# A linear-attention kernel fused with a mixture-of-experts block: the opening put in hand order on four engines, with dummy products, and the loop's order of work rewritten

## The chip, the cores and the metric

The kernel runs on one core of one Trainium2 chip. Times are device microseconds (us) of one execution. Repeated executions of one kernel mostly agree within about 0.5%. Each execution has a state, fast or slow (slow: more than 1.5% above the fastest of its kernel). A "span" is the time from the first to the last instruction in the one execution that was profiled; it is 1.5 to 2 us shorter than that execution's time.

## The reference

RWKV-6 attention over four sequences, eight heads, 768 positions and head size 48. Its output, as 3072 rows of 384, goes through a two-layer block with a squared ReLU.

```python
def _attn_ref(r, k, v, w, u):
    state = zeros(B, H, D, D)
    for t in range(S):
        kt, vt, rt, wt = k[:, :, t], v[:, :, t], r[:, :, t], w[:, :, t]
        cur = einsum('bhd,bhe->bhde', u[None] * kt, vt)
        y[:, :, t] = einsum('bhd,bhde->bhe', rt, state + cur)
        state = wt[:, :, :, None] * state + einsum('bhd,bhe->bhde', kt, vt)
    return y

def _moe_ref(x, w_in, w_out):          # 3072x384, 384x2048, 2048x384
    r = np.maximum(x @ w_in, 0.0)
    return (r * r) @ w_out
```

## The kernel before

The attention is cut into 24 steps of 128 positions (six per sequence). A step is a chain across engines, and the letters name its TensorE parts:

- `c`: sums of the logarithms of w. ScalarE takes `Ln` before and `Exp` after it, then VectorE multiplies r and k by the result (`rdec`).
- `t`: transposes of `rdec`, copied out by VectorE (`rkT`).
- `p`: products of keys and receptances, masked by VectorE (`pmT`).
- `s`: the state update, finished by VectorE and GpSimd.
- `y`: the step's output. VectorE adds the bonus term `vq` (`y_sb`).
- `x`: transposes of `y_sb`, copied by ScalarE into `xT`, the input of the second part.

Beside the chain GpSimd makes the bonus: `ku`, `qprod`, then VectorE's reduction `q`, then `vq` again on GpSimd. It needs the step's k from memory, and nothing in the step needs it before `y_sb`.

The block behind it ("MoE" in the code) is cut into units, and `F` puts one into the order of TensorE. A first-layer unit, called A here, is six products of 256 columns; ScalarE takes it out of PSUM (`rl`) and VectorE squares it (`gt`). A second-layer unit, called B, is four products of 384 columns; after four B units ScalarE takes the sum out of PSUM (`o_sb`). Either unit takes TensorE about 0.655 us (0.66 us for an A and 0.65 us for a B from one start to the next, at 158.35 us in the timeline of the steady loop below). There are 192 of them. A has two PSUM buffers, B has one; `cp` and `y` (one buffer of 2 x 512 columns each) and `tr` (one) are the rest.

```python
    ps_m1 = ctx.enter_context(tc.tile_pool(name="ps_m1", bufs=2, space=PSUM))
    ps_m2 = ctx.enter_context(tc.tile_pool(name="ps_m2", bufs=1, space=PSUM))
    # ... cut ...
    def fill(_):                                   # the F of the order
        if not fills and coming:
            fills.extend(coming.popleft()[1])      # a new block, before its time
        if not fills and held and flush[0]:
            fills.extend(held.popleft())           # second-layer units alone
        if fills:
            fills.popleft()()
        if coming:
            coming[0][0] -= 1
            if coming[0][0] <= 0:                  # LAG = 2 fills after its x
                fills.extend(coming.popleft()[1])

    def finish(step):                              # the x of the order
        st_yt(step)
        if step in blocks:
            m1s, m2s = moe_block(*blocks[step])
            old = held.popleft() if held else []
            held.append(m2s)
            units = []
            for i in range(max(len(m1s), len(old))):
                units += m1s[i:i + 1] + old[i:i + 1]   # A B A B ...
            coming.append([LAG, units])
    # ... cut ...
    with tc.manual_schedule(engines={nc.tensor.engine}):
        st_prep(0)
        run("c0 t0 p0 s0 i0 c1 i1 y0 t1 x0 p1 s1 i2 y1 i3 x1 O0 O1 O2 O3")
        ahead(PF - 1)
        run("F F F F F F c2 F F t2 o0 p2 s2 o1 y2 o2 x2 o3 F F F F F F F F c3 F F F F t3 s3")
        flush[0] = False
        for t in range(3, NSTEP):
            f = ["F F"] * 4 if t > 8 else ...      # cut: fewer in the first steps
            run(f"c{t + 1} {f[0]}" + (f" x{t - 1}" if t > 3 else "") +
                f" {f[1]} t{t + 1} p{t} {f[2]} s{t + 1} {f[3]} y{t}")
        run(f"F F x{NSTEP - 1}")
        flush[0] = True
        while fills or held or coming:
            fill(0)
```

Only TensorE runs in the order of the text; the order of VectorE, ScalarE and GpSimd is chosen automatically when the kernel is built. The loop is pipelined by a step: `c`, `t` and `s` of step t+1 stand beside `p` and `y` of step t. And `flush[0] = False` keeps second-layer units back until there are first-layer units to alternate with.

## Time and profile before

| | |
|---|---|
| time, median of 4 executions (range) | 233.99 us (233.26 to 234.39) |
| span, mean granted clock of TensorE | 232.5 us, 0.955 |
| TensorE busy, 120 to 190 us | 69.78 of 70 us |
| steady period of a step (start of `rdec`, steps 10 to 22) | 7.49 us |
| start of `y_sb` of step 8, of step 23 | 96.8 us, 209.1 us |

The page cuts the span into 40 slices of 5.8 us. Each digit is a busy share in tenths, and the second line is the granted clock of TensorE in tenths of full speed:

```profile
PE   0145694794787999989999999999999999999984
PEclk9999997589569999999999999999999999999999
DMA  7999998999999999998785561010001000101001
```

TensorE has holes for 80 us, in which the loads bring the digit of the DMA engines to 7 to 9, and then almost none. The table of windows gives the same by stage. Its columns are the stretch, its length, busy time of PE (TensorE), PEld (its weight loads), DVE (VectorE), ACT (ScalarE) and POOL (GpSimd) with the count of instructions, the granted clock, the DMA share and GB/s:

```profile
0.00:45.00 45.00, 21.62 (x203) 15.05 (x204) 18.12 (x35) 24.65 (x34) 14.69 (x27) 0.92 1.04 244
45.00:60.00 15.00, 11.57 (x109) 8.18 (x108) 6.40 (x13) 7.20 (x15) 8.87 (x10) 0.84 1.17 183
60.00:84.00 24.00, 19.30 (x249) 13.79 (x249) 17.40 (x33) 12.31 (x26) 12.88 (x16) 0.83 1.13 198
84.00:120.00 36.00, 34.56 (x407) 25.56 (x403) 29.24 (x55) 22.65 (x47) 19.31 (x22) 1.00 0.97 177
120.00:190.00 70.00, 69.78 (x813) 51.71 (x809) 54.43 (x99) 45.48 (x94) 24.93 (x30) 1.00 0.24 57
```

So up to about 84 us there is something to win for TensorE, and afterwards the kernel is as good as its work. Two lines each of the timelines of ScalarE, VectorE and TensorE show the opening. The columns are start, length, engine, line, operation, and in brackets the idle time before it and who ended it:

```profile
6.66 0.51 ACT L151 CAST v_bf<-v_raw 128x384 bf16<-128x384 f32 x1 [4.64 <-DMA v_raw<-in_v_dram]
7.08 0.52 ACT L149 ACTIVATE lw_buf_149<-w_raw 128x384 bf16<-128x384 f32 x1
...
10.15 0.55 DVE L160 TENSOR_REDUCE q<-qprod 128x8 f32<-128x384 f32 x1 [7.64 <-POOL qprod L158]
10.62 0.94 DVE L177 TENSOR_TENSOR rdec_buf_155<-rk_raw,cp 128x768 bf16<-128x768 f32 x1
...
26.52 1.44 PE L272 MATMUL m_370<-xT,wi_sb 128*128 128x256 bf16 x6 [0.57 <-ACT xT L256]
...
32.10 0.82 PE L272 MATMUL m_420<-xT,wi_sb 128*128 128x256 bf16 x6
```

The first `Ln` stands behind a cast of v that waited for its load. The first `rdec`, which the whole chain waits for, stands behind a bonus reduction that nobody needs yet (this alone costs 0.2 us, as its `Exp` ended at 10.41 us). The first A units run at about half speed: the first takes 1.44 us, and the next two start 1.28 us apart (27.75 and 29.03 us), against 0.82 us at 32.10 us and 0.66 us from one start to the next in the loop. In the steady loop, A and B alternate (L272 is A, L287 is B), with no idle time in brackets:

```profile
158.35 0.82 PE L272 MATMUL m_2601<-xT,wi_sb 128*128 128x256 bf16 x6
159.01 0.81 PE L287 MATMUL m_2549<-wo_sb,gt 128*128 128x384 bf16 x4
159.66 0.33 PE L255 MATMUL tr<-ident,y_sb 128*128 128x128 bf16 x3
159.82 0.82 PE L272 MATMUL m_2620<-xT,wi_sb 128*128 128x256 bf16 x6
160.48 0.81 PE L287 MATMUL m_2549<-wo_sb,gt 128*128 128x384 bf16 x4
```

### The profile page before, as it was taken

Reading aid. Unit: us, or ns where it says so; the run is one execution under the profiler, and the core shown is the slowest. Engines: PE = TensorE matmul, PEld = TensorE weight load, DVE = VectorE, ACT = ScalarE, POOL = GpSimd, SP = SyncE. Lnnn points to the kernel's source line nnn. Section 1 sums busy time; section 2 is a strip of 40 time slices with the busy share of each in tenths; the row PEclk is TensorE's granted clock in tenths of the full one; section 3 lists DMA queues with packets and bytes.
Section 4 is the critical chain, followed back from the end, with each engine's and each line's share of the span. In section 5 each row is a group of like instructions: output and inputs, shape, how many; then the busy total and the mean of one; then the engine's idle time right before and its main releaser. Section 6 shows DMA issues by size and latency. Waiting matters only on the chain.

```text
span 232.5 us, 5432 instructions
## 1 busy us (share of the span) xinstructions
PE 194.8 (84%) x2120; PEld 141.3 (61%) x2120; DVE 143.0 (61%) x264; ACT 131.4 (57%) x249; POOL 81.2 (35%) x105
## 2 busy tenths in 40 slices
PE   0145694794787999989999999999999999999984
PEld 0023472663465677767777777777777777777742
DVE  2244356235567688796879878987677756753210
ACT  2338479274245558547655775567755664455530
POOL 4450410547525855357626563431211120000000
PEclk9999997589569999999999999999999999999999
DMA  7999998999999999998785561010001000101001
GB/s 137 206 344 280 327 295 163 190 171 189 187 206 216 174 199 194 220 184 166 141 167 113 110 126 37 34 36 3 35 34 38 35 3 34 37 34 37 34 34 68
DMA packets 107176, 30.42 MB, mean 131 GB/s; under 512 B 100368, under 2 KB 105616, under 8 KB 107152
## 3 DMA queue, kind: packets, MB, share of 16 engines
q1 hardware_dynamic: 107152, 30.09, 63.0%
q8 instruction: 16, 0.26, 0.5%
q14 instruction: 8, 0.07, 0.1%
HBM read 25.36 MB, written 4.72 MB: 129 GB/s over the span
## 4 chain that ended last, share of the span: by engine, by line
PE 56%; SPq 14%; DVE 8%; DMA 7%; POOL 6%; issue 4%; ACT 3%; POOLq 0%; DVEq 0%; ACTq 0%
SPq L68 13%; PE tr L188 4%; DMA rk_raw<-in_k_dram 4%; PE cp L220 2%; DVE pmT L223 2%; POOL qprod L158 2%; POOL ku L157 2%; DVE rkT L189 2%; DMA u_bc<-in_u_dram 2%; DMA v_raw<-in_v_dram 2%; DVE gt L277 1%; PE y L234 1%; PE tr L255 1%; PE cp L171 1%; PE m_3691 L287 1%
## 5 line engine op out<-in xcount | busy, mean ns | idle before, releaser
L277 DVE TENSOR_TENSOR gt<-rl 128x512 bf16<-128x512 f16 x96 | 48.1, 509 | 34.2 <-ACT rl L276 33.8
L272 PEld LDWEIGHTS <-wi_sb 128*128 128x128 bf16 x624 | 57.2, 102 | 15.4 <-issue 3.4
L287 PEld LDWEIGHTS <-gt 128*128 128x128 bf16 x384 | 37.4, 99 | 18.6 <-issue 2.7
L208 POOL TENSOR_TENSOR S<-t_state,a_c 128x192 bf16<-128x192 f32 x20 | 10.5, 525 | 72.6 <-DVE t_state L206 56.3
L223 DVE TENSOR_TENSOR pmT<-cp,tri_strict 128x512 bf16<-128x512 f32 x48 | 30.7, 679 | 2.5 <-PE cp L220 2.5
L162 POOL TENSOR_TENSOR vq<-v_raw,q 128x384 f32<-128x384 f32 x24 | 20.0, 833 | 32.8 <-DVE y_sb L245 18.9
L160 DVE TENSOR_REDUCE q<-qprod 128x8 f32<-128x384 f32 x24 | 13.2, 549 | 21.5 <-POOL qprod L158 13.9
L157 POOL TENSOR_TENSOR ku<-rk_raw,u_bc 128x384 f32<-128x384 f32 x24 | 24.4, 1018 | 4.6 <-DMA u_bc<-in_u_dram 4.6
L158 POOL TENSOR_TENSOR qprod<-rk_raw,ku 128x384 f32<-128x384 f32 x24 | 24.4, 1018 | 3.1 <-DVE q L160 1.3
L151 ACT CAST v_bf<-v_raw 128x384 bf16<-128x384 f32 x24 | 12.2, 510 | 15.4 <-PE y L234 8.8
L189 DVE COPY rkT<-tr 128x1024 bf16<-128x1024 bf16 x24 | 16.4, 685 | 5.7 <-PE tr L188 5.4
L175 ACT ACTIVATE cp<-cp 128x768 f32<-128x768 f32 x24 | 19.2, 799 | 0.5 <-DVE q L160 0.2
L245 DVE TENSOR_TENSOR y_sb<-vq,y 128x384 bf16<-128x384 f32 x24 | 13.2, 551 | 2.2 <-PE y L234 1.1
L256 ACT COPY xT<-tr 128x384 bf16<-128x384 bf16 x24 | 11.4, 476 | 3.4 <-PE tr L255 3.3
L220 PE MATMUL cp<-rkT 64*128 64x128 bf16 x192 | 10.6, 237 | 3.0 <-DVE rkT L189 3.0
L234 PEld LDWEIGHTS <-pmT 128*128 128x128 bf16 x192 | 8.9, 101 | 6.8 <-DVE pmT L223 4.4
L234 PE MATMUL y<-v_bf,pmT 128*128 128x48 bf16 x192 | 10.6, 191 | 2.8 <-DVE pmT L223 2.7
L177 DVE TENSOR_TENSOR rdec_buf_159<-rk_raw,cp 128x768 bf16<-128x768 f32 x8 | 7.6, 952 | 6.5 <-ACT cp L175 5.1
L255 PE MATMUL tr<-ident,y_sb 128*128 128x128 bf16 x72 | 8.6, 234 | 2.4 <-DVE y_sb L245 1.6
L220 PEld LDWEIGHTS <-rkT 64*128 64x128 bf16 x192 | 6.0, 101 | 6.2 <-DVE rkT L189 3.4
L188 PE MATMUL tr<-ident,rdec_buf_157 128*128 128x128 bf16 x64 | 5.7, 242 | 4.7 <-DVE rdec_buf_157 L177 4.7
L255 PEld LDWEIGHTS <-y_sb 128*128 128x128 bf16 x72 | 6.0, 103 | 5.9 <-DVE y_sb L245 2.8
(295 smaller groups left out, 362.8 us busy)
## 6 DMA issues: line engine op xcount, KB each, us to landing
w_raw<-in_w_dram SPq DMA_DIRECT2D x24, 192.0 KB, 4.4
rk_raw<-in_r_dram SPq DMA_DIRECT2D x24, 192.0 KB, 4.5
rk_raw<-in_k_dram SPq DMA_DIRECT2D x24, 192.0 KB, 4.6
v_raw<-in_v_dram SPq DMA_DIRECT2D x24, 192.0 KB, 4.0
out_dram<-o_sb SPq DMA_DIRECT2D x24, 192.0 KB, 2.0
w_st<-in_moe_w_in_dram SPq DMA_DIRECT2D x4, 768.0 KB, 8.0
w_st<-in_moe_w_out_dram SPq DMA_DIRECT2D x4, 768.0 KB, 9.3
u_bc<-in_u_dram SPq DMA_DIRECT2D x1, 192.0 KB, 4.2
```

Source lines behind the costliest of these rows:

```text
L68: nc.sync.dma_start(out=dst, in_=src[b, :, c * C:(c + 1) * C, :].rearrange("h c d -> c h d"))
L157: nc.gpsimd.tensor_mul(ku[:], st["rk_raw"][:, 1], u_bc[:])
L158: nc.gpsimd.tensor_mul(qprod[:], st["rk_raw"][:, 0], ku[:])
L162: nc.gpsimd.tensor_mul(vq[:], st["v_raw"][:], q[:, :, None].to_broadcast([C, H, D]))
L175: nc.scalar.activation(cs[:, :, 0:DM], cs[:, :, 0:DM], AF.Exp)
L189: nc.vector.tensor_copy(rkT[:], ps_tr[:])
L220: nc.tensor.matmul(ps_p[:, e, p * C:(p + 1) * C], rkT[rows, 1, p, :], rkT[rows, 0, p, :], start=True, stop=True)
L223: nc.vector.tensor_mul(pmT[:, e], ps_p[:, e].rearrange("p (a t) -> p a t", a=HP), tri_strict[:, None, :].to_broadcast([C, HP, C]))
L234: nc.tensor.matmul(ps_y[:, e, p * D:(p + 1) * D], st["pmT"][:, e, p, :], st["v_bf"][:, 2 * p + e, :], start=(p == 0), stop=(c == 0), skip_ ...
L272: nc.tensor.matmul(ps1[:, j, :], wi_sb[:, kk, n * 128:(n + 1) * 128], xT[:, kk, t0:t0 + width], start=(kk == 0), stop=(kk == KT - 1))
L277: nc.vector.tensor_mul(hold["gt"][:, g * ng:(g + 1) * ng, :], rl[:], rl[:])
L287: nc.tensor.matmul(ps2[:], gt[:, n, mt * 128:(mt + 1) * 128], wo_sb[:, n, :], start=(n == 0), stop=(n == NT - 1))
```

## The change

The intent was to shorten the opening. VectorE, ScalarE and GpSimd are put in hand order too for steps 0 to 3. The casts of the weights are cut into slices and shared by ScalarE (`i`, `o`) and VectorE (`I`, `O`). TensorE's idle time is filled with 43 dummy products (`W`), meant to keep its clock up. MoE blocks of the steps 2, 3, 4 and 23 cover one step. Two things come along with this in the loop: it is no longer pipelined by a step, and the `flush` flag is gone, so second-layer units are used as soon as the fills run empty.

```diff
-    def cast_wi(g):
-        nc.scalar.copy(wi_sb[:, :, g * GW:(g + 1) * GW], w_st.pop(("i", g))[:])
+    def cast(dst, src, by_act):
+        for j in range(dst.shape[1]):
+            if by_act:
+                nc.scalar.copy(dst[:, j], src[:, j])
+            else:
+                nc.vector.tensor_copy(dst[:, j], src[:, j])
 # ... cut: the old cast_wo; cast_wi and cast_wo now call cast; st_prep is split into st_lw (l) and st_v (v), st_bonus into st_bonus (b)
 #     and st_q (q), st_cum into st_cum (c) and st_rd (r), one letter each ...
-    blocks = {1: (0, 256), 2: (2 * C, 128), 3: (3 * C, 128)}
-    for step in range(5, NSTEP, 2):
+    blocks = {1: (0, 256)}
+    for step in range(2, NLEAD):                    # NLEAD = 5
+        blocks[step] = (step * C, 128)
+    for step in range(NLEAD + 1, NSTEP, 2):
         blocks[step] = ((step - 1) * C, 256)
+    if (NSTEP - NLEAD) % 2:
+        blocks[NSTEP - 1] = ((NSTEP - 1) * C, 128)
-    flush = [True]
-        if not fills and held and flush[0]:
+        if not fills and held:
             fills.extend(held.popleft())
+    def keep_warm(n):
+        ps = ps_m2.tile([C, 512], FP32, name="m2")
+        for _ in range(n):
+            nc.tensor.matmul(ps[:], warm[:, 0:C], warm[:], start=True, stop=True)
-    # ... cut: the opening and the loop shown above ...
+    with tc.manual_schedule(engines={E.PE}):
+        with tc.manual_schedule(engines={E.DVE, E.Activation, E.Pool}):
+            run("W10 l0 c0 r0 v0 b0 W6 t0 W2 q0 p0 l1 s0 W2 y0 W1 c1 b1 x0 r1 v1 W6 t1"
+                " W2 q1 p1 i0 s1 W2 y1 W2 x1 I1 F i2 F F I3 F J0 F F l2 c2 F F b2 r2 v2"
+                " J1 J2 J3 H4 W4 t2 W2 q2 p2 o0 s2 W2 y2 W2 x2 O1 F F F F o2 F F O3 F l3 c3"
+                " F F b3 r3 v3 F F t3 F q3 p3 F s3 F y3 l4")
+        for t in range(4, NSTEP):
+            f = FEW if t < NFEW else "F F;F F;F F;F;F".split(";")   # FEW: 6 fills, t < 8
+            run(f"c{t} r{t} b{t} H{t + PF - 1} {f[0]} x{t - 1} v{t} {f[1]} t{t} q{t} {f[2]}"
+                f" p{t} {f[3]} s{t} {f[4]} y{t}" + (f" l{t + 1}" if t + 1 < NSTEP else ""))
```

More of the change, by code (lines that the diff above doesn't have):

```diff
@@ L46 @@
     LAG = 2
+    NLEAD = 5
+    NFEW = 8
+    FEW = "F;F;F F;F;F".split(";")
     nc.scalar.preload_act_table_set("natural_log_exp_and_others")
@@ L97, in load_wo, with cast_wi, cast_wo, load_u @@
             in_=moe_w_out[g * 512:(g + 1) * 512, :].rearrange("(a p) d -> p a d", p=128))
-    def cast_wi(g):
-        nc.scalar.copy(wi_sb[:, :, g * GW:(g + 1) * GW], w_st.pop(("i", g))[:])
-    def cast_wo(g):
-        nc.scalar.copy(wo_sb[:, g * 4:(g + 1) * 4, :], w_st.pop(("o", g))[:])
-    loads = {0: attn_load(0)}
-    u_bc = consts.tile([C, H, D], FP32)
-    nc.sync.dma_start(
-        out=u_bc[:],
-        in_=bass.AP(tensor=u.tensor, offset=u.offset,
-                    ap=[[0, C]] + [list(x) for x in u.ap]))
-    loads[1] = attn_load(1)
+    def cast(dst, src, by_act):
[4 more added lines that the diff above has]
+                nc.vector.tensor_copy(dst[:, j], src[:, j])
+    def cast_wi(g, by_act):
+        cast(wi_sb[:, :, g * GW:(g + 1) * GW], w_st.pop(("i", g)), by_act)
+    def cast_wo(g, by_act):
+        cast(wo_sb[:, g * 4:(g + 1) * 4, :], w_st.pop(("o", g)), by_act)
+    loads = {}
+    u_bc = consts.tile([C, H, D], FP32)
+    def load_u():
+        nc.sync.dma_start(
+            out=u_bc[:],
+            in_=bass.AP(tensor=u.tensor, offset=u.offset,
+                        ap=[[0, C]] + [list(x) for x in u.ap]))
+    def load_step(step):
+        loads[step] = attn_load(step)
+    load_step(0)
+    load_u()
+    load_step(1)
     for g in range(4):
         load_wi(g)
-    loads[2] = attn_load(2)
+    load_step(2)
     tri_strict = consts.tile([C, C], BF16)
@@ L125 @@
     nc.vector.memset(ones_col[:], 1.0)
+    warm = consts.tile([C, 512], BF16)
+    nc.vector.memset(warm[:], 0.0)
     NLW = 3
@@ L142, with st_lw, st_v @@
     S_of = {}
-    def st_prep(step):
-        ld = loads.pop(step)
-        st = states[step] = dict(ld)
+    def st_lw(step):
+        st = states[step] = dict(loads.pop(step))
         lw = st["lw"] = lw_bufs[step % NLW]
-        nc.scalar.activation(lw[:, :, 0:D], ld["w_raw"][:], AF.Ln)
+        nc.scalar.activation(lw[:, :, 0:D], st["w_raw"][:], AF.Ln)
+    def st_v(step):
+        st = states[step]
         v_bf = st["v_bf"] = a_mid.tile([C, H, D], BF16, name="v_bf", bufs=3)
-        nc.scalar.copy(v_bf[:], ld["v_raw"][:])
+        nc.scalar.copy(v_bf[:], st["v_raw"][:])
     def st_bonus(step):
@@ L155, in st_bonus, with st_q @@
         ku = a_mid.tile([C, H, D], FP32, name="ku")
-        qprod = a_mid.tile([C, H, D], FP32, name="qprod")
+        qprod = st["qprod"] = a_mid.tile([C, H, D], FP32, name="qprod")
         nc.gpsimd.tensor_mul(ku[:], st["rk_raw"][:, 1], u_bc[:])
         nc.gpsimd.tensor_mul(qprod[:], st["rk_raw"][:, 0], ku[:])
+    def st_q(step):
+        st = states[step]
         q = a_small.tile([C, H], FP32, name="q")
-        nc.vector.reduce_sum(q[:], qprod[:], axis=AX.X)
+        nc.vector.reduce_sum(q[:], st["qprod"][:], axis=AX.X)
         vq = st["vq"] = a_mid.tile([C, H, D], FP32, name="vq", bufs=3)
@@ L166, in st_cum @@
         lw = st["lw"]
-        cs = ps_cp.tile([C, 2, 512], FP32, name="cp")
+        cs = st["cs"] = ps_cp.tile([C, 2, 512], FP32, name="cp")
         for p in range(HP):
@@ L175, in st_cum, with st_rd @@
         nc.scalar.activation(cs[:, :, 0:DM], cs[:, :, 0:DM], AF.Exp)
+    def st_rd(step):
+        st = states[step]
         rdec = st["rdec"] = rdec_bufs[step % NRD]
@@ L178, in st_cum @@
             rdec[:, :, :, 0:D], st["rk_raw"][:],
-            cs[:, :, 0:DM].rearrange("p a (h d) -> p a h d", h=H))
+            st.pop("cs")[:, :, 0:DM].rearrange("p a (h d) -> p a h d", h=H))
     def st_tr(step):
@@ L335, in ahead @@
         while asked[0] <= min(last, NSTEP - 1):
-            loads[asked[0]] = attn_load(asked[0])
+            load_step(asked[0])
             asked[0] += 1
-    def cum(step):
-        if step < NSTEP:
-            st_cum(step)
-            if step + 1 < NSTEP:
-                st_prep(step + 1)
-            if step > 1:
-                ahead(step + PF)
-    def tr(step):
-        if step < NSTEP:
-            st_tr(step)
-            st_bonus(step)
-    def su(step):
-        if step < NSTEP:
-            st_su(step)
-    ops = {"c": cum, "t": tr, "p": st_p, "s": su, "y": st_y, "x": finish,
-           "F": fill,
-           "i": cast_wi, "o": cast_wo, "O": load_wo}
+    ops = {"l": st_lw, "v": st_v, "c": st_cum, "r": st_rd, "b": st_bonus, "q": st_q,
+           "t": st_tr, "p": st_p, "s": st_su, "y": st_y, "x": finish, "F": fill,
+           "W": keep_warm, "J": load_wo, "H": ahead,
+           "i": lambda g: cast_wi(g, True), "I": lambda g: cast_wi(g, False),
+           "o": lambda g: cast_wo(g, True), "O": lambda g: cast_wo(g, False)}
     def run(text):
@@ L362, in run @@
             ops[tok[0]](int(tok[1:] or 0))
-    with tc.manual_schedule(engines={nc.tensor.engine}):
-        st_prep(0)
-        run("c0 t0 p0 s0 i0 c1 i1 y0 t1 x0 p1 s1 i2 y1 i3 x1 O0 O1 O2 O3")
-        ahead(PF - 1)
-        run("F F F F F F c2 F F t2 o0 p2 s2 o1 y2 o2 x2 o3 F F F F F F F F c3 F F F F t3 s3")
-        flush[0] = False
-        for t in range(3, NSTEP):
-            f = ["F F"] * 4 if t > 8 else ["F F", "F F", "F F", "F"] if t > 5 else ["F"] * 4 if t == 3 else ["F", "", "F", ""]
-            run(f"c{t + 1} {f[0]}" + (f" x{t - 1}" if t > 3 else "") +
-                f" {f[1]} t{t + 1} p{t} {f[2]} s{t + 1} {f[3]} y{t}")
+    E = mybir.EngineType
+    with tc.manual_schedule(engines={E.PE}):
+        with tc.manual_schedule(engines={E.DVE, E.Activation, E.Pool}):
+            run("W10 l0 c0 r0 v0 b0 W6 t0 W2 q0 p0 l1 s0 W2 y0 W1 c1 b1 x0 r1 v1 W6 t1"
[3 rows of a table added]
+        for t in range(4, NSTEP):
+            f = FEW if t < NFEW else "F F;F F;F F;F;F".split(";")
+            run(f"c{t} r{t} b{t} H{t + PF - 1} {f[0]} x{t - 1} v{t} {f[1]} t{t} q{t} {f[2]}"
+                f" p{t} {f[3]} s{t} {f[4]} y{t}" + (f" l{t + 1}" if t + 1 < NSTEP else ""))
         run(f"F F x{NSTEP - 1}")
-        flush[0] = True
         while fills or held or coming:
```

## The prediction

> **What bounds the kernel now.** Two regimes. From 120 to 209 us TensorE is busy 88.8 of 89 us (table of windows), about 7.55 us per step of 128 rows. Before 83.7 us it is busy only 52.2 us, partly at half clock: six products of a MoE block took 1.44-1.49 us until 30 us and 0.82 us later; the granted clock of 40-50 and 60-70 us was 0.61 and 0.58. DMA is saturated until about 106 us (page, slices); from 36 us on a step's loads are issued every 4.0-4.5 us and land 4.0-4.6 us later: step 3 is complete at about 40 us, step 4 at 44, step 6 at 52-53.
>
> **What the change does.** (1) Hand order for VectorE, ScalarE, GpSimd in steps 0-3: the first Ln no longer stands behind the cast of v (6.66 us), the first rdec product no longer behind the reduction q (10.15 us). Following the chain with the trace's durations, rdec of step 0 starts near 7.5 instead of 10.6, the first MoE product near 21 instead of 26.5, the transposed rows of step 2 come near 35 instead of 42. (2) Dummy products, 43 of 512 columns, keep TensorE warm[...]. They sit in gaps and save 4-6 us of cold MoE. (3) Single-step blocks for steps 2-4 and 23 cost nothing: 12 products of 128 columns were spaced 0.67 us, six of 256 columns 0.66. A halved last block saves 0.6 us of tail. (4) Casts keep their total. (5) Fills: 45 MoE units come ahead of step 8 instead of 32; 13 x 0.655 = 8.5 us moved into the opening.
>
> **What takes some back.** After step 3 VectorE's built order has the reductions q of steps 4, 5 and 6 ahead of rdec of step 4. q of step 6 needs its k (landed about 52), then ku, S, qprod (2.5 us on GpSimd): rdec of step 4 cannot start before about 55 us (before: 57.2), with a TensorE hole of some 4 us[...]. The early lead is largely lost to DMA; the fills done in it stay. Second, the steady order is no longer pipelined by one step, and fills come as eight first-layer units, then eight second-layer ones. In the first-layer stretch VectorE has 8 us of work per 7.5 us; between p and y stand 1.6 us of TensorE work for a 1.3 us mask product, and a unit waits for its evictor behind the 0.8 us Exp. I estimate 0.2-0.5 us lost per step, 3-8 us in 16 steps.
>
> **Sum.** 8.5 (fills) + 1.2 (attention products of step 7 already done) + 2 (rdec of step 4) + 0.6 (tail) less about 4 = 8 us off 234.3.
>
> **Prediction: 226 us, 219 to 231 eight times in ten. Faster by over 2%: 0.76; within 2%: 0.21; slower: 0.03.**
>
> **What would show it.** First MoE product at 20-22 us, six in 0.8 us; rdec of step 4 at 53-57 us, released by q or k of step 6, after a TensorE hole; step period after step 8 of 7.6-8.0 us, with waits on relu evictions and masked products (pmT); last attention product near 209 us or later, then a MoE tail of 13 us instead of 20.
>
> **What would make it wrong.** k of step 6 earlier, or no steady stalls (then 219). Or the eight-and-eight fills stall more than 0.5 us a step, or outputs in the DMA queue hold back loads (then over 230).

That dummies keep TensorE fast was not yet shown by a run then; hl_nowarm below gives the measure, and the 4 to 6 us put on it were the estimate from before's trace (six products in 1.44 to 1.49 us instead of 0.82, clock 0.61 and 0.58).

## The result and the profile after

| | before | after |
|---|---|---|
| time, median (range) | 233.99 us (233.26 to 234.39) | 236.82 us (236.54 to 237.22) |
| span, mean granted clock | 232.5 us, 0.955 | 235.2 us, 0.993 |
| first A unit, six products | 26.52 us, 1.44 us long | 20.21 us, 0.81 us long |
| steady period of a step | 7.49 us | 8.11 us |
| start of `y_sb` of step 8, of step 23 | 96.8, 209.1 us | 95.1, 217.4 us |

The ratio is 1.013 (95% interval 1.009 to 1.016). A ratio here is the mean time of a kernel's fast executions over that of the fast executions of the kernel before in the same rounds, so it is not quite the ratio of the medians quoted. The change made the kernel 1.3% slower, clear of the noise but within 2%, on a predicted gain of 3.4%. All outputs, here and in every experiment below, agree with the reference.

The page's slices and the windows of after answer to those above:

```profile
PE   7776768497987788989989989999989999999984
PEclk9999999979999999999999999999999999999999
```

```profile
0.00:45.00 45.00, 32.98 (x297) 18.44 (x301) 25.40 (x52) 21.91 (x44) 17.05 (x29) 1.00 1.00 243
...
60.00:84.00 24.00, 19.16 (x264) 13.74 (x264) 19.60 (x33) 13.02 (x27) 14.01 (x16) 1.00 1.13 195
...
120.00:190.00 70.00, 65.49 (x728) 47.27 (x727) 50.16 (x93) 42.98 (x88) 21.10 (x26) 1.00 0.35 73
```

The first row has 33 us of TensorE work in place of 22, part of it dummies. The clock is what the change wanted: from 60 to 84 us it is 1.00, where it was 0.83. The last row is what nobody wanted. TensorE is idle for 4.51 us of 70, where it was idle for 0.22 us before. The view of waits, for TensorE from 120 to 190 us, lists nothing for before. For after it lists these among others (total, times, longest, in us; L299 is A, L314 is B):

```profile
PE y L261 <- DVE pmT L250: 0.5, 2, 0.3
PE m_2028 L299 <- ACT rl L303: 0.5, 1, 0.5
PE m_2618 L299 <- ACT rl L303: 0.5, 1, 0.5
...
PE cp L247 <- DVE rkT L216: 0.4, 2, 0.2
PE m_2688 L314 <- ACT o_sb L318: 0.3, 1, 0.3
```

The timeline of TensorE over one step shows where they stand:

```profile
153.21 0.82 PE L299 MATMUL m_2591<-xT,wi_sb 128*128 128x256 bf16 x6
153.86 0.82 PE L299 MATMUL m_2601<-xT,wi_sb 128*128 128x256 bf16 x6
154.52 0.33 PE L282 MATMUL tr<-ident,y_sb 128*128 128x128 bf16 x3
155.32 0.82 PE L299 MATMUL m_2618<-xT,wi_sb 128*128 128x256 bf16 x6 [0.47 <-ACT rl L303]
155.97 0.81 PE L314 MATMUL m_2628<-wo_sb,gt 128*128 128x384 bf16 x4
...
160.29 0.81 PE L314 MATMUL m_2688<-wo_sb,gt 128*128 128x384 bf16 x4 [0.34 <-ACT o_sb L318]
```

A units now come together, eight of A and then eight of B, because every step consumes exactly the eight units that it makes, the queue of fills runs empty in between, and without the flag an empty queue is filled with B units alone. The third A of the stretch shown needs a PSUM buffer that ScalarE has not emptied (0.47 us). The fifth B in a row needs the only B buffer (0.34 us). With the alternating order of before, each buffer had a unit of the other kind in which to be emptied.

The second new thing lies between 42 and 57 us. The first fence is ScalarE's timeline and the second TensorE's; the third is VectorE's a little later:

```profile
44.84 0.52 ACT L167 ACTIVATE lw_buf_155<-w_raw 128x384 bf16<-128x384 f32 x1 [1.85 <-DMA w_raw<-in_w_dram]
...
45.46 0.80 ACT L199 ACTIVATE cp<-cp 128x768 f32<-128x768 f32 x1
46.16 0.49 ACT L318 ACTIVATE o_sb<-m_601 128x384 f32<-128x384 f32 x1
```

```profile
43.48 0.81 PE L314 MATMUL m_601<-wo_sb,gt 128*128 128x384 bf16 x4
46.70 2.80 PE L314 MATMUL m_688<-wo_sb,gt 128*128 128x384 bf16 x12 [2.41 <-ACT o_sb L318]
```

```profile
54.40 0.55 DVE L272 TENSOR_TENSOR y_sb<-vq,y 128x384 bf16<-128x384 f32 x1 [0.34 <-PE y L268]
56.59 0.55 DVE L184 TENSOR_REDUCE q<-qprod 128x8 f32<-128x384 f32 x1 [1.64 <-POOL qprod L179]
57.06 0.95 DVE L204 TENSOR_TENSOR rdec_buf_159<-rk_raw,cp 128x768 bf16<-128x768 f32 x1
```

The `Ln` at 44.84 us writes the third of the three buffers in turn, whose earlier use was step 2, so it belongs to step 5. It waited 1.85 us for step 5's w, and the `Exp` of step 3 at 45.46 us stood behind it, though its products were done by 43.7 us (from TensorE's timeline). The B sum that had to leave PSUM stood behind both, hence TensorE's hole of 2.41 us. The reduction at 56.59 us is `q` of step 6, read from the built order of VectorE. It waited 1.64 us, with `rdec` of step 4 behind it, whose `Exp` had ended at 55.99 us: `rdec` itself was held for 1.07 us. The load wasn't what came last here: step 6's k had landed at 52.0 us, but GpSimd, busy with `vq` and `qprod` of earlier steps, began `ku` at 54.14 us. In these fences both engines ran their instructions in the order in which they stand: the `Exp` began only behind the `Ln` that had waited 1.85 us, and `rdec` only behind the reduction that had waited 1.64 us. In both the automatic order of the loop has put an operation of a later step, which isn't ready (on ScalarE it waits for a load, on VectorE for GpSimd), ahead of one that TensorE needs now. The hand order of the opening did not keep it out: hand-ordered instructions keep their order among themselves, and here an automatic one (the `Ln` of step 5 at 44.84 us) stands between them, ahead of the `Exp` of step 3.

### A ledger of the lead

Since one kernel is pipelined and the other not, `rdec` of the same step is not the same point of progress. The addition `y_sb` is. With the count of MoE units that stand ahead of it in TensorE's order (counted in the program text, fills that find nothing left out), the profiled executions give:

| kernel | `y_sb` of step 8 | units ahead of it | step 8 to 23 (120 units) | step 23 to the end | span |
|---|---|---|---|---|---|
| before | 96.8 us | 44 | 112.3 us | 23.4 us | 232.5 us |
| after | 95.1 us | 53 | 122.4 us | 17.8 us | 235.2 us |

At step 8 after was 1.7 us and 9 units ahead; at 0.655 us a unit that is a lead of 7.6 us. It then lost 10.1 us in the steady loop, and its end was 5.6 us shorter for the 9 units already done. The sum is -1.7 + 10.1 - 5.6 = 2.8 us, and the spans differ by 2.7 us.

Even `y_sb` is not quite the same point. The pipelined kernel has done `c`, `t` and `s` of the next step by then, except at step 23, which has no next one. These take TensorE 1.1 us (0.44, 0.45 and 0.24 us from one start to the next in after, 151 to 158 us). So after's lead at step 8 is rather 6.5 us and its steady loss 9.0 us; the sum stays the same. The period agrees: 15 steps of 0.63 us are 9.4 us.

### The profile page after: what moved, and what is told of

It reads as the page before. It is cut to its first block, busy times and chain, and to the rows that moved or that the text cites. A ratio compares the mean times of both kernels' runs of the same rounds, so it can differ in the third digit from the quotient of the medians.

```text
span 235.2 us, 5615 instructions
## 1 busy us (share of the span) xinstructions
PE 201.6 (86%) x2208; PEld 138.8 (59%) x2211; DVE 151.1 (64%) x279; ACT 127.2 (54%) x255; POOL 81.3 (35%) x105
## 4 chain that ended last, share of the span: by engine, by line
PE 49%; DVE 16%; issue 11%; POOL 8%; ACT 8%; DMA 5%; SPq 3%; POOLq 0%; DVEq 0%; ACTq 0%
DVE pmT L250 6%; DVE gt L304 4%; PE tr L215 3%; POOL ku L178 3%; POOL qprod L179 3%; ACT rl L303 3%; DMA rk_raw<-in_r_dram 3%; PE cp L247 3%; SPq L71 3%; ACT o_sb L318 2%; DVE rkT L216 2%; DMA u_bc<-in_u_dram 2%; PE y L261 2%; PE cp L195 1%; PE y L268 1%
## 5 line engine op out<-in xcount | busy, mean ns | idle before, releaser
L299 PEld LDWEIGHTS <-wi_sb 128*128 128x128 bf16 x672 | 56.6, 97 | 19.1 <-issue 9.6
L304 DVE TENSOR_TENSOR gt<-rl 128x512 bf16<-128x512 f16 x96 | 49.3, 529 | 16.2 <-ACT rl L303 15.8
L314 PEld LDWEIGHTS <-gt 128*128 128x128 bf16 x384 | 35.7, 98 | 26.9 <-issue 8.3
L250 DVE TENSOR_TENSOR pmT<-cp,tri_strict 128x512 bf16<-128x512 f32 x48 | 31.7, 685 | 6.6 <-PE cp L247 6.5
L186 POOL TENSOR_TENSOR vq<-v_raw,q 128x384 f32<-128x384 f32 x24 | 20.0, 833 | 30.3 <-DVE y_sb L272 14.3
L204 DVE TENSOR_TENSOR rdec_buf_157<-rk_raw,cp 128x768 bf16<-128x768 f32 x8 | 7.6, 950 | 10.1 <-ACT cp L199 10.1
L247 PE MATMUL cp<-rkT 64*128 64x128 bf16 x192 | 9.5, 219 | 3.1 <-DVE rkT L216 3.1
L247 PEld LDWEIGHTS <-rkT 64*128 64x128 bf16 x192 | 5.4, 94 | 10.7 <-DVE rkT L216 7.6
L198 ACT ACTIVATE a_c<-cp 128x4 f32<-128x4 f32 x24 | 4.1, 173 | 13.5 <-PE cp L196 13.5
L204 DVE TENSOR_TENSOR rdec_buf_159<-rk_raw,cp 128x768 bf16<-128x768 f32 x8 | 7.6, 949 | 3.9 <-ACT cp L199 3.9
L204 DVE TENSOR_TENSOR rdec_buf_161<-rk_raw,cp 128x768 bf16<-128x768 f32 x8 | 7.6, 948 | 2.0 <-ACT cp L199 2.0
```

Of the source, the lines that this page charges most:

```text
L186: nc.gpsimd.tensor_mul(vq[:], st["v_raw"][:], q[:, :, None].to_broadcast([C, H, D]))
L204: nc.vector.tensor_mul(rdec[:, :, :, 0:D], st["rk_raw"][:], st.pop("cs")[:, :, 0:DM].rearrange("p a (h d) -> p a h d", h=H))
L247: nc.tensor.matmul(ps_p[:, e, p * C:(p + 1) * C], rkT[rows, 1, p, :], rkT[rows, 0, p, :], start=True, stop=True)
L250: nc.vector.tensor_mul(pmT[:, e], ps_p[:, e].rearrange("p (a t) -> p a t", a=HP), tri_strict[:, None, :].to_broadcast([C, HP, C]))
L299: nc.tensor.matmul(ps1[:, j, :], wi_sb[:, kk, n * 128:(n + 1) * 128], xT[:, kk, t0:t0 + width], start=(kk == 0), stop=(kk == KT - 1))
L304: nc.vector.tensor_mul(hold["gt"][:, g * ng:(g + 1) * ng, :], rl[:], rl[:])
```

## The experiments

Each edit is against after unless it says otherwise. "Before" was run again beside each group, with medians of 233.9 to 234.4 us. Groups ran on different chips, so that times of different groups compare less well than their ratios. All results are of timed rounds; periods and single lines are of one profiled execution. Each kernel has four timed executions; hold_lag, hand_all and hand_pipe had one slow one each, which is left out of their ratios and medians. hand_all's profile is of the slowest of its three fast executions (240.0 us at a mean granted clock of 0.985; the others took 236.8 and 237.0 us at 0.998 and 1.000). Its windows show a clock of 0.50 from 12.6 to 15.9 us and from 46.7 to 50.0 us (six dummy products took 2.58 us at 13.67 us; in outq the same six took 1.46 us), so lines of its opening come later than in the others; in the loop, from 120 to 190 us, its clock was 1.00.

| kernel | median us | ratio to before (95%) | steady period us | `y_sb` of step 8 | step 8 to 23 |
|---|---|---|---|---|---|
| after | 236.8 | 1.013 (1.009 to 1.016) | 8.11 | 95.1 | 122.4 |
| hold | 243.5 | 1.041 (1.033 to 1.049) | 8.29 | 93.3 | 125.2 |
| pipe | 238.7 | 1.019 (1.014 to 1.024) | 8.15 | 96.7 | 121.3 |
| pipe_hold | 234.7 | 1.001 (0.994 to 1.008) | 7.68 | 97.0 | 113.3 |
| oldopen | 239.4 | 1.022 (1.017 to 1.027) | 8.11 | 96.3 | 122.8 |
| hold_lag | 233.4 | 0.998 (0.992 to 1.004) | 7.70 | 89.8 | 116.8 |
| outq | 241.7 | 1.034 (1.032 to 1.037) | 8.03 | 98.0 | 122.7 |
| hand8 | 242.9 | 1.039 (1.036 to 1.042) | 8.19 | 97.8 | 124.8 |
| nowarm | 237.8 | 1.018 (1.012 to 1.023) | 8.12 | 94.5 | 122.8 |
| hand_all | 237.0 | 1.016 (1.008 to 1.024) | 8.50 | 92.5 | 127.7 |
| hand_lag | 226.0 | 0.965 (0.961 to 0.969) | 7.49 | 86.0 | 113.8 |
| hand_pipe | 225.5 | 0.965 (0.959 to 0.972) | 7.49 | 89.6 | 110.5 |
| cap | 232.7 | 0.995 (0.987 to 1.003) | 7.61 | 91.2 | 115.6 |
| hl_oldopen | 231.1 | 0.988 (0.986 to 0.990) | 7.50 | 92.0 | 113.9 |
| bef_hand | 230.6 | 0.986 (0.983 to 0.989) | 7.48 | 94.4 | 110.5 |
| hl_nowarm | 229.2 | 0.983 (0.977 to 0.988) | 7.50 | 90.0 | 113.9 |

### Is it the bursts, or the loop that is no longer pipelined?

The main theory for the steady loss was that units of one kind in a burst wait for their evictor. The rival was that the loop, no longer pipelined by a step, leaves too little between `p`, the mask and `y`. The first three kernels change one or both.

**hold** brings the flag back and leaves the rest of after:

```diff
-        if not fills and held:
+        if not fills and held and flush[0]:
             fills.extend(held.popleft())
 # and, around the loop:
+        flush[0] = False
         for t in range(4, NSTEP):
 # ...
         run(f"F F x{NSTEP - 1}")
+        flush[0] = True
```

> The changed kernel, but from step 4 on second-layer MoE units are held back until the next block's first-layer units can be alternated with them, as in the kernel before; the attention order stays unpipelined. Theory burst (eight first-layer units in a row overload VectorE and ScalarE): the period between the rdec products of steps 10 and 22 falls from 8.11 to about 7.6 us. Theory order (no pipelining by a step, so short distances p to y and c to t): it stays at 8.0 or more. Total is muddied by the backlog that alternation needs (some empty fills in steps 5 to 9): 228 to 236 under burst, 236 to 242 under order.

It was the slowest of all, 243.5 us. The waits on PSUM are nearly gone, but another has come. The view of waits for TensorE, 120 to 190 us:

```profile
PE m L299 <- ACT xT L283: 4.9, 4, 1.2
PE m L314 <- ACT o_sb L318: 0.6, 3, 0.2
```

Every second step the fills run out just before `x`, and the first A unit of the new block stands directly behind the transposes whose copy `xT` it needs: 1.2 us each time. Before still has units left at that point, and `LAG` puts two of them in between. So alternation needs a backlog, and after has used it up.

**pipe** restores the pipelined order and keeps the bursts:

```diff
-        for t in range(4, NSTEP):
-            f = FEW if t < NFEW else "F F;F F;F F;F;F".split(";")
-            run(f"c{t} r{t} b{t} H{t + PF - 1} {f[0]} x{t - 1} v{t} ... y{t} l{t + 1}")
+        cnt = {3: (1, 1, 1, 1), 4: (1, 2, 2, 1), 5: (1, 2, 2, 1), 6: (1, 2, 2, 1), 7: (1, 2, 2, 1)}
+        for t in range(3, NSTEP):
+            f = ["F " * n for n in cnt.get(t, (2, 2, 2, 2))]
+            # n = t + 1; the parts a, b, d are empty at the end, cut
+            run(f"c{n} r{n} H{n + PF - 1} l{n + 1} v{n + 1} {f[0]} x{t - 1} {f[1]}"
+                f" t{n} b{n} q{n} p{t} {f[2]} s{n} {f[3]} y{t}")
```

> The changed kernel with the loop order of the kernel before from step 3 on (cumulative sums and transposes one step ahead of masked product and y), but the fills still come as eight first-layer and eight second-layer units. Theory order: period of steps 10 to 22 falls to 7.5-7.7 us, total about 227. Theory burst: it stays at 8.0 or more, total about 235.

It took 238.7 us with a period of 8.15 us, and TensorE still waited 2.3 us for `o_sb` and 2.1 us for `rl` in the same 70 us. The rival falls: the pipelined order with bursts is no better than the plain order with bursts.

**pipe_hold** has both, the order of pipe with the flag of hold, and eleven fills fewer than pipe in the steps 3 to 8, so that a backlog stays.

```diff
+        cnt = {3: (0, 0, 0, 0), 4: (1, 1, 1, 1), 5: (1, 2, 1, 1), 6: (1, 1, 1, 1),
+               7: (1, 2, 2, 1), 8: (1, 2, 2, 1)}
+        flush[0] = False
```

> New opening, and both the pipelined order and the alternating fills of the kernel before from step 3 on. Both theories: period of steps 10 to 22 at 7.5-7.6 us. If the new opening is worth anything by itself, the total is clearly under 234: I expect 224 to 229. If its lead is lost to the loads anyway, 231 to 235.

It took 234.7 us, period 7.68 us. The stretch from step 8 to 23 fell to 113.3 us, almost that of before. But the kernel is only level with before, although its opening is the new one. By step 8 (97.0 us) no lead was left.

**hold_lag** settles it the other way round: after's plain order, the flag, and ten fills fewer in steps 4 to 8 (22 in the text instead of 32), so that a backlog exists.

```diff
+        flush[0] = False                              # and True at the end, as in hold
         for t in range(4, NSTEP):
-            f = FEW if t < NFEW else "F F;F F;F F;F;F".split(";")
+            f = ["F " * n for n in {4: (1, 1, 0, 1, 0), 5: (1, 1, 1, 1, 0), 6: (1, 1, 1, 1, 0),
+                 7: (1, 1, 1, 1, 1), 8: (1, 1, 2, 1, 1)}.get(t, (2, 2, 2, 1, 1))]
```

> As hold (unpipelined attention order, alternating fills), but with 5 fewer fills in steps 4 to 8, so that a backlog of units remains when a block is requested and its first product no longer follows right on the transpose of x (hold waited 0.55 us per step for ScalarE's copy xT). Theory burst with exhausted fills: period of steps 10 to 22 falls to 7.5-7.7 us, waits of second-layer units for o_sb and of first-layer units for rl near zero. Theory order: it stays over 7.9 us with waits on pmT and rkT.

It took 233.4 us (231.9 to 235.1, a wide scatter), period 7.70 us, without pipelining. The waits for `rl` and `o_sb` are gone from TensorE's list between 120 and 190 us, and 1.1 us for `rdec` and 0.6 us for `rkT` remain, which are waits on VectorE. So most of the steady loss is made by bursts of one kind and by the missing backlog, and the loop that is no longer pipelined is not needed to explain it. The 0.2 us a step that remain against before's 7.49 us are these waits on VectorE; hand_lag below, which is not pipelined either, has 7.49 us. The gaps in after were 0.3 to 0.5 us each; what closed them was no buffer more but another order in front of the same buffers.

### What is the opening worth under after's loop?

**oldopen** puts the opening of before in front of after's loop (whole casts on ScalarE, only TensorE in hand order, no dummies):

```diff
-                nc.scalar.copy(dst[:, j], src[:, j])  # and the slices on VectorE
+        nc.scalar.copy(dst, src[:])
-        with tc.manual_schedule(engines={E.DVE, E.Activation, E.Pool}):
-            run("W10 l0 c0 r0 v0 b0 W6 t0 ... y3 l4")
+        run("l0 v0 c0 r0 l1 v1 t0 b0 q0 p0 s0 i0 c1 r1 l2 v2 i1 y0 t1 b1 q1 x0 p1 s1 i2 y1 i3 x1 J0 J1 J2 J3 H7"
+            " F F F F F F c2 r2 l3 v3 H10 F F t2 b2 q2 o0 p2 s2 o1 y2 o2 x2 o3 F F F F F F F F c3 r3 H11"
+            " F F F F t3 b3 q3 s3 F p3 F y3 l4")
```

> The counterpart: the instruction order of the opening before (casts unsliced on ScalarE, no dummy products, only TensorE in hand order), then the unpipelined loop of the changed kernel. Period of steps 10 to 22 stays at 8.1 us. If the new opening is worth its 6 to 10 us, the total is 241 to 247; if its lead is lost to the loads, 235 to 239.

It took 239.4 us. The new opening is worth 2.5 us at the end (239.4 - 236.8), and in the profiled executions 1.3 us at step 8 (96.3 against 95.1), with the same 53 units done. Seen from before, 6.3 us of after's lead of 7.6 at step 8 are there without the new opening: 0.5 us and 9 units. They come mostly from more fills per step: at `y` of step 3 after is ahead by 2 units (22 against 20), at that of step 8 by 9. The comparison is not quite clean, as the automatic order came out differently with the old opening: in oldopen no reduction held `rdec` of step 4.

**nowarm** leaves out the dummy products (one column each time is left, so that the buffers keep their turns):

```diff
-        for _ in range(n):
-            nc.tensor.matmul(ps[:], warm[:, 0:C], warm[:], start=True, stop=True)
+        for _ in range(min(n, 1)):
+            nc.tensor.matmul(ps[:, 0:1], warm[:, 0:C], warm[:, 0:1], start=True, stop=True)
```

> The changed kernel with each run of dummy products reduced to one product of one column. If the clock matters: [...]rdec of step 3 later by 2 to 4 us, total up by 1 to 3 us. If the loads swallow it anyway: total within 0.7 us of the changed kernel.

It took 237.8 us, 0.9 us more than after by the medians of two groups, which the intervals (1.012 to 1.023, 1.009 to 1.016) don't show as a difference. `rdec` of step 3 came 2.3 us later (48.55 against 46.28 us), but that of step 4 not (56.63 against 57.06): whatever the dummies won had been lost by then. What held step 4 was not the same in both: in nowarm `rdec` of step 4 followed its `Exp` at once, so the automatic order had changed with this edit too.

### What eats the lead in steps 4 to 8?

The main theory was VectorE's automatic order: `q` of later steps, standing ahead of `rdec`. The rival was that outputs in the queue that issues the loads hold the loads back. In after that queue issues nothing from 44.28 to 46.67 us and from 49.04 to 52.13 us, in front of an output both times.

**outq** issues the outputs of the first five steps from ScalarE's queue instead:

```diff
-                    nc.sync.dma_start(
+                    (nc.scalar if t0 < NLEAD * C else nc.sync).dma_start(
                         out=out[t0 + mt * 128:t0 + (mt + 1) * 128, :], in_=o_sb[:])
```

> The changed kernel, the first five outputs issued from ScalarE's queue instead of the loads' queue. Theory queue (loads of steps 6 and 7 stand behind outputs that wait for ScalarE: 2.4 and 3.1 us at 44-52 us): k of step 6 lands 2-5 us earlier, rdec of step 4 starts at 53-55 instead of 57.1 us, total 1.5 to 3 us lower (234 to 235.5). If the outputs do not matter, within 0.7 us of the changed kernel's 236.8.

The loads did come earlier: those of step 8 were issued from 52.6 us instead of 57.2. Yet the kernel took 241.7 us. The automatic order of VectorE had changed with the edit, and at 81 us VectorE waited nearly three us in the `q` of step 11, with `rdec` of step 7 behind it (held for 1.8 us after its `Exp`). That reduction's k had landed at 73.3 us; it waited for GpSimd. VectorE's timeline:

```profile
81.17 0.55 DVE L184 TENSOR_REDUCE q<-qprod 128x8 f32<-128x384 f32 x1 [2.96 <-POOL qprod L179]
81.64 0.94 DVE L204 TENSOR_TENSOR rdec_buf<-rk_raw,cp 128x768 bf16<-128x768 f32 x1
```

`rdec` of step 4 came 0.4 us earlier than in after. So loads that come earlier brought next to nothing here. That the outputs' issue now takes ScalarE's time (0.34 to 1.67 us each) is a second new thing that the run doesn't separate. Separate issuers brought the loads forward by 4.6 us (step 8), and the time was 3.4% longer than before's; the changed order stands in the trace, its share of the loss is not tested by itself.

**hand8** extends the hand order on all engines to step 7:

```diff
+        with tc.manual_schedule(engines={E.DVE, E.Activation, E.Pool}):
+            steps(4, 8)           # the loop's text, as in after
+        steps(8, NSTEP)
```

> The changed kernel, hand order of VectorE, ScalarE and GpSimd kept on to step 7, so that no reduction q or Ln of a later step stands ahead of rdec. Theory order-ahead (q of step 6 holds rdec of step 4): rdec of step 4 at 51-54 us instead of 57.1, total 2 to 4 us lower. If the hold was elsewhere, rdec of step 4 stays at 56 to 58 us.

`rdec` of step 4 came at 53.3 us instead of 57.1, as the theory wanted. Then, where the automatic order begins, VectorE waited twice for 2.51 us, first in front of `pmT` of step 8 and then of `rdec` of step 9 (held for 1.7 us after its `Exp`). This is its timeline at the end of it; the reduction is that of step 14, and `rdec` is that of step 9:

```profile
100.83 0.55 DVE L184 TENSOR_REDUCE q<-qprod 128x8 f32<-128x384 f32 x1 [2.51 <-POOL qprod L179]
101.30 0.94 DVE L204 TENSOR_TENSOR rdec_buf<-rk_raw,cp 128x768 bf16<-128x768 f32 x1
```

From step 8 to step 9 `rdec` took 14.3 us (87.0 to 101.3). The kernel took 242.9 us. Hand order on part of the loop only moved the place at which later steps' operations crowd in.

**hand_all** therefore keeps hand order to the end, with after's bursts. `l{t+1}` moves ahead of the transposes:

```diff
+        with tc.manual_schedule(engines={E.DVE, E.Activation, E.Pool}):
+            for t in range(4, NSTEP):
+                f = FEW if t < NFEW else "F F;F F;F F;F;F".split(";")
+                nxt = f"l{t + 1}" if t + 1 < NSTEP else ""
+                run(f"c{t} r{t} b{t} H{t + PF - 1} {f[0]} x{t - 1} v{t} {nxt} {f[1]} t{t} q{t} {f[2]}"
+                    f" p{t} {f[3]} s{t} {f[4]} y{t}")
```

> The changed kernel with VectorE, ScalarE and GpSimd in hand order to the end (each q after its own rkT; the next Ln moved ahead to the transpose of x), fills still in bursts. hand8 only postponed the reductions q of later steps: they then held rdec of step 9. Theory order-ahead: without any q ahead, rdec of step 8 comes at 80-84 us (changed kernel 88.4) and the total falls by 4 to 8 us to 229-233; the period stays near 8.1 us because of the bursts. If order-ahead is not what eats the lead: total 235 to 239.

It took 237.0 us (236.8 to 240.0), which by the ratios is no different from after (1.016 against 1.013). By its own expectation this speaks against the automatic order. But even in the profiled execution it was at 92.5 us at step 8 with the same 53 units, 2.6 us ahead of after, and lost that in the loop, where its period was 8.50 us: there the bursts cost even more in this order. hand_lag below decides. TensorE's waits, 120 to 190 us:

```profile
PE y L261 <- DVE pmT L250: 2.5, 8, 0.5
PE m L314 <- ACT o_sb L318: 1.4, 4, 0.3
```

**cap** tries to hold the automatic order back by fewer buffers, on top of hold_lag:

```diff
-        q = a_small.tile([C, H], FP32, name="q")
+        q = a_small.tile([C, H], FP32, name="q", bufs=1)
-        vq = st["vq"] = a_mid.tile([C, H, D], FP32, name="vq", bufs=3)
+        vq = st["vq"] = a_mid.tile([C, H, D], FP32, name="vq", bufs=2)
```

> hold_lag with automatic order, but q single-buffered and vq double-buffered, so that a reduction can stand at most two steps ahead of the data in use. Order-ahead in a weaker form: rdec of step 8 earlier than hold_lag's 84.4 by 1 to 3 us, total 230 to 233; if the new waits on the single buffer cost as much, 233 to 236.

It took 232.7 us, ratio 0.995 against 0.998 of hold_lag: no difference that the intervals show. VectorE still waited 1.26 us at 54 us in front of `rdec` of step 4, now in a `q` that waits for GpSimd's `vq`, that is, for the single buffer: one wait was exchanged for another.

### Both together

**hand_lag** is hand_all with the fills and the flag of hold_lag. Nothing else is new in it.

```diff
+        flush[0] = False
+        with tc.manual_schedule(engines={E.DVE, E.Activation, E.Pool}):
+            for t in range(4, NSTEP):
+                f = [...]                             # the fills of hold_lag
+                nxt = f"l{t + 1}" if t + 1 < NSTEP else ""
+                run(...)                              # the text of hand_all
```

> hand_lag is hand_all plus the alternating fills with a backlog of hold_lag: both causes mended together. Period of steps 10 to 22 at 7.5-7.6 us, rdec of step 8 at 79-82 us, total 222 to 228, faster than both kernels. If one of the two readings is wrong: 230 or more.

It took 226.0 us (225.1 to 226.6), ratio 0.965: 3.5% faster than before and 10.8 us less than after. Here are the lines that answer to those of after: the window of the steady loop, the page's slices of PE and its clock, and `rdec` of step 4 on VectorE's timeline:

```profile
120.00:190.00 70.00, 69.98 (x814) 50.93 (x812) 51.65 (x103) 44.32 (x93) 30.46 (x36) 1.00 0.30 64
```

```profile
PE   7777578787877889999999999999999999999973
PEclk9999999999999999999999999999999999999999
```

```profile
53.04 0.96 DVE L204 TENSOR_TENSOR rdec_buf<-rk_raw,cp 128x768 bf16<-128x768 f32 x1 [0.99 <-ACT cp L199]
```

TensorE is busy for 69.98 of 70 us and its list of waits in that window is empty. `rdec` of step 4 is now released by its own `Exp`, as it should be. The step-3 hole of TensorE shrank from 2.41 to 0.90 us (read from its timeline at 45.38 us). Of the 4.0 us by which `rdec` of step 4 comes earlier than in after (53.04 against 57.06 us), 1.3 us are there at step 3, about 1.0 us is what the reduction had held it, and 1.7 us lie between, where after's clock was 0.50 from 48 to 51 us and hand_lag's 1.00. (In hand_all's profiled execution a hole of 0.58 us at the same place was followed by a clock of 0.50 too, so in these three the length of this one hole does not tell the cases apart.) These 1.7 us are in some measure luck: two of hand_lag's four executions had a mean clock of 0.992 instead of 1.000 and took 226.4 and 226.6 us instead of 225.1 and 225.7. In the ledger: 10.8 us ahead of before at step 8 with the same 44 units, 1.5 us lost from step 8 to 23 (1.1 us of both being the `c`, `t` and `s` of above), nothing lost at the end, 9.2 us in all, which is the difference of the spans.

The four kernels with the same opening and the plain order form a square:

| | bursts (after's fills) | alternating with a backlog |
|---|---|---|
| automatic order in the loop | 236.8 | 233.4 |
| hand order in the loop | 237.0 | 226.0 |

Hand order alone changes nothing that the scatter lets one see, the fills alone win 3.4 us, both together win 10.8 us. The two faults hide each other. With bursts, the profiled hand_all lost in the loop what hand order had won before step 8; with the automatic order, hold_lag's `rdec` of step 4 was held 1.65 us after its `Exp` (hand_lag: 0.03 us), and TensorE had waits for `rdec` and `rkT` in the loop.

**hand_pipe** is the same with the pipelined order, that is, pipe_hold with hand order in the loop, `b` moved up next to `r` and `q` behind `p`.

```diff
-        for t in range(4, NSTEP):                     # the loop of after
+        cnt = {...}                                   # the fills of pipe_hold, the flag too
+        with tc.manual_schedule(engines={E.DVE, E.Activation, E.Pool}):
+            for t in range(3, NSTEP):
+                # n = t + 1; the parts are empty at the end, cut
+                run(f"c{n} r{n} b{n} H{n + PF - 1} {f[0]} x{t - 1} l{n + 1} v{n + 1} {f[1]}"
+                    f" t{n} p{t} q{n} {f[2]} s{n} {f[3]} y{t}")
```

> pipe_hold (pipelined order, alternating fills) with full hand order. Under order-ahead the holds on rdec of step 4 and 9 (q6, q12) vanish: total 223 to 229 against 234.7 of pipe_hold. Otherwise 233 to 236.

It took 225.5 us, ratio 0.965. So pipelining is worth nothing measurable here once the other two are mended.

### What is left of the opening, then?

Three more kernels ask this of the mended loop. **hl_oldopen** is hand_lag with the opening of oldopen, **bef_hand** is hand_pipe with the opening of oldopen, and **hl_nowarm** is hand_lag with the edit of nowarm.

```diff
 # hl_oldopen, against hand_lag; bef_hand, against hand_pipe, has the same two edits
 # (its opening text ends in "t3 b3 q3 s3 l4 v4", as the pipelined loop holds p3 and y3):
-                nc.scalar.copy(dst[:, j], src[:, j])  # and the slices on VectorE
+        nc.scalar.copy(dst, src[:])
-            run("W10 l0 c0 r0 v0 b0 W6 t0 ... y3 l4")
+        run("l0 v0 c0 r0 l1 v1 t0 b0 q0 p0 s0 i0 ... F F F F t3 b3 q3 s3 F p3 F y3 l4")
 # hl_nowarm, against hand_lag:
-        for _ in range(n):
-            nc.tensor.matmul(ps[:], warm[:, 0:C], warm[:], start=True, stop=True)
+        for _ in range(min(n, 1)):
+            nc.tensor.matmul(ps[:, 0:1], warm[:, 0:C], warm[:, 0:1], start=True, stop=True)
```

> hand_lag with the opening of the kernel before (automatic order of VectorE, ScalarE, GpSimd in steps 0 to 3, whole casts on ScalarE, no dummy products). If the new opening is worth what the prediction said once nothing eats it (rdec of step 3 at 45 instead of 52 us): 4 to 7 us slower than hand_lag, 230 to 233. If the loads or the backlog absorb it: within 2 us of hand_lag, 226 to 228.

> hand_pipe with the opening of the kernel before, that is nearly the kernel before with only its loop's VectorE, ScalarE and GpSimd put in hand order. If hand order alone carries the gain: 226 to 229, clearly under 234. If the new opening carries it: 231 to 235.

> hand_lag without its dummy products (one column left of each run). If the clock in the opening matters once the lead is kept: rdec of step 2 later by 2 us as in nowarm, and the total up by 1.5 to 3 us; if not, within 0.7 us of hand_lag.

They took 231.1, 230.6 and 229.2 us, on another chip than hand_lag and hand_pipe, with ratios of 0.988, 0.986 and 0.983 against 0.965. The opening is worth 5.0 us in the plain loop (231.1 - 226.0; by the ratios 2.3% of 234 us, 5.4 us) and 5.1 us in the pipelined one (by the ratios 4.9 us), and the dummies make 3.2 us of the former (by the ratios 4.1 us). In the profiled executions the gain of the opening is 6.15 us at `rdec` of step 3 (51.12 against 44.97), and 6.0 us at `y_sb` of step 8 (92.0 against 86.0): in the mended loop all of it arrives, and 4.0 us of it are the dummies' (hl_nowarm: 90.0 us at step 8). In after's loop 1.3 us arrived.

The dummies show in one line. TensorE's timeline with the first A units of the kernel, three of six products each, in hl_nowarm and then in hand_lag:

```profile
21.31 4.00 PE L299 MATMUL m<-xT,wi_sb 128*128 128x256 bf16 x18 [0.57 <-ACT xT L283]
```

```profile
20.41 2.31 PE L299 MATMUL m<-xT,wi_sb 128*128 128x256 bf16 x18 [0.57 <-ACT xT L283]
```

The same 18 products take 4.00 us without dummies before them and 2.31 us with them. How much work before them is needed for that no run here measures.

bef_hand also shows that part of the final gain of 3.5% is not the change's at all: with the old opening the loop in hand order is 1.4% faster than before.

## Why the prediction was wrong

The sign was wrong. Two terms of its sum failed, the lead at step 8 and the steady loss, by about 5 us each. Point by point:

- **The opening itself was right.** The first A unit was predicted at 20 to 22 us with six products in 0.8 us; it came at 20.21 us in 0.81 us. `rdec` of step 0 was predicted near 7.5 us, and came at 7.49 us.
- **The place where the lead would be lost was right, the reason in half.** "q of step 6 ... rdec of step 4 cannot start before about 55 us": it started at 57.06 us (range given 53 to 57), behind that reduction, with a hole (2.41 us) and a clock of 0.50 (48 to 51 us) earlier. But step 6's k, landed at 52.0 us as predicted, was not what came last: GpSimd took it up 2.1 us later. And the sum had counted 2 us won at this `rdec`; it was 0.2 us (57.24 against 57.06). What the prediction missed is that the automatic order also reached into the hand-ordered opening, on ScalarE in step 3 (the hole of 2.41 us), and that the fault goes on in later steps (`rdec` held for 0.50 us at step 8, 0.36 us at step 10).
- **"13 x 0.655 = 8.5 us moved into the opening" failed.** The count compared unlike points: the loop before is pipelined, so its step 8 begins one step earlier in the text. Ahead of `c` of step 8 stand 45 units in after and 30 in before (the prediction has 32), but after's `rdec` of step 8 comes 4.7 us later (88.44 against 83.72 us), where the sum took it to be 2 us earlier. Counted up to the same `y`, it is 9 units, 5.9 us. With 1.7 us of time, and without the 1.1 us of `c`, `t` and `s`, the lead at step 8 was 6.5 us, where the sum had 8.5 + 1.2 + 2 = 11.7.
- **"I estimate 0.2-0.5 us lost per step, 3-8 us in 16 steps" failed by as much.** The mechanism was named rightly, eight of A and then eight of B with units waiting for their evictor (0.47 us for `rl`, 0.34 us for `o_sb` in the timeline of after). Its size was not. The period grew by 0.63 us (8.11 against 7.49), and from step 8 to 23 9.0 us were lost (10.1 us as the ledger's table has it), where the sum had put in about 4. TensorE's idle time, 4.51 of 70 us against 0.22, makes 0.50 us of the 0.63 us a step (4.29 us over 8.63 steps). No single wait accounts for the other 0.13 us.
- **"A halved last block saves 0.6 us of tail" didn't show.** The end from the last `y_sb` was 17.8 us (the text had 13), 5.6 us shorter than before for 9 units (5.9 us) already done, so nothing was saved beyond them.
- **The sum.** Predicted 11.7 - 4 + 0.6, about 8 us to the good; found 6.5 - 9.0 - 0.3, or 2.8 us to the bad. Of the miss of 11 us, 5 are the steady loop, 5 the lead, 1 the end.
- **"What would make it wrong" held half of it**: it named fills that stall more than 0.5 us a step, and that came true. It also named outputs that hold back loads. The gaps are in the trace, but outq, with earlier loads, was no faster; it is no test of their whole worth, because the order changed with it.

Left open: why the automatic order came out as it did in outq and hand8, beyond the lines shown; how the 4.6 us that `y_sb` lost against before between the steps 4 and 8 (32.1 us against 27.5, while 25 units were done instead of 23) divide among its waits; what the clock of 0.50 after the hole at 44 us cost by itself; and how much of hand_lag's scatter against the kernels of the last group is owed to another chip.

## What to carry to other kernels

A faster opening is worth only what the loop behind it passes on: look at the loop's bottleneck first, and count the lead at a point that means the same in both kernels. Where two kinds of units share one engine and have as few PSUM buffers as here (two and one), alternate them and leave a small backlog, because consuming exactly what each step makes leaves bursts (8.11 us a step) or a wait at each block (8.29 us), and a backlog gave 7.70 us, with hand order 7.49 us, with the same buffers. Read the built order of the other engines for operations of later steps that stand ahead of the critical one (they waited 1.64 us on VectorE and 1.85 us on ScalarE in after, 2.51 us in hand8, 2.96 us in outq); put either the whole loop in hand order or expect the fault at the seam, and test mends that may hide each other together.
